# Sparse attention and feed forward: P by V behind the next scores, key copies and conversions dealt out in pieces

## The chip, the cores and the metric

The kernel runs on one core of a Trainium2 chip. A core has five engines that run at the same time, each with its own queue of instructions in program order: TensorE (PE; its weight loads are a row of their own, PEld), VectorE (DVE), ScalarE (ACT), GpSimd (POOL) and SyncE (SP). They wait for each other by semaphores. Data moves by DMAs, which SP, ACT and POOL issue. The metric is the device time of one execution in microseconds (us); less is better.

## What is computed

Block-sparse attention for 4 batches, 8 heads, 768 positions and 64 values a head, then a layer norm and a feed forward with a residual. In blocks of 32 positions, a query block sees its neighbours, the first and the last block, and three sampled blocks; the first and the last query block see all.

```python
scores = scale * np.matmul(q, k.transpose(0, 1, 3, 2))
...
mask = np.abs(blk_i - blk_j) <= window
mask = mask | (blk_i == 0) | (blk_j == 0) | (blk_i == n_blocks - 1) | (blk_j == n_blocks - 1)
for qb in range(n_blocks):
    for kb in sampled_blocks[qb]:
        mask[qb * block:(qb + 1) * block, kb * block:(kb + 1) * block] = True
scores = np.where(mask, scores, -1000000000.0)
...
attn = attn / (np.sum(attn, axis=-1, keepdims=True) + 1e-09)
return np.matmul(attn, v).astype(np.float32)
...
xn = (x - mu) / np.sqrt(var + 1e-06) * g_ln
ch = np.maximum(xn @ w_ch1, 0.0) @ w_ch2
return (x + ch).astype(np.float32)
```

The feed forward goes from 512 to 2048 and back.

## The kernel before

**Numbers.** Every fp32 operand of a matmul is held as two fp16 parts, a high and a low one (`qx`/`ql`, `pt[..., 0/1, :]`, `hh`/`hl`, `w1h`/`w1l`, `w2h`/`w2l`), and each product is three matmuls. To convert is a copy on ACT (high) and a subtraction on DVE (low): `convert_k` (L227, L228), `convert_v` (L241, L242), `convert_q` (L264 to L266), `convert_w` (L173 to L187; its ACT and DVE parts stand in the lists `whigh` and `wlow`, which `high()` and `low()` empty).

**Steps and units.** A batch has three units of two tiles of 128 positions: tiles (1, 2), (3, 4) and (0, 5) (`ORDER`). A step is four heads of one tile: 48 sparse steps, and 16 dense ones (`dense=True`) for the query blocks 0 and 23. A unit with tiles 0 and 5 has eight steps, the others four: 64 steps in all (`NS`). When a unit's steps are done its two tiles are normalised (`layer_norm`) and its feed forward (`ffn`) becomes available: 192 up matmuls (L523, eight groups of 24, each in one of three accumulators of the pool `ps_f`) and 96 down matmuls (L548). `hidden` takes a group's relu to fp16 (hh on ACT, L535; hl on DVE, L536); it is put into the program one group late (`late`).

**One step.** `scores` (L324) is 96 small matmuls (32 stationary columns, 64 or 96 moving ones); `softmax_max` (L368) and `softmax_exp` (L377); P is then split and transposed, in the first eight steps (`NPE`) by TensorE (`turn`, L382), later by SyncE's DMA transposes (`split_low`, L398); `attn_v` is P by V, 96 small matmuls (L431; dense: L458), with `finish` on DVE.

**Gathers.** The sampled keys are copied by ACT from the converted keys (`gather_k`, L281, twelve copies a step, by block numbers in registers). V is written in fp16 to a scratch tensor in DRAM (`vdr`) and fetched for a step by `gather_v` into one of three buffers `vg`: direct DMAs on SP (L290, L294) and one indirect DMA on POOL for each query block (L298, three or four a step). POOL holds little else. A buffer is free when the P by V of three steps before is done; that is what the indirect DMAs wait for.

**The order.** It is written out by hand, one iteration of the main loop for each step (L751 to L872). An iteration has a share of feed forward (`need`, `nff`), cut into eight parts, and `run(n)` puts n of its pieces into the program. `hook(i, p)` runs what was planned for point p of iteration i: conversions (`item`), V gathers (`at`), then loads that have room (`pump`). In the first eight iterations scores of step i + 1 come after P by V of step i - 1 and two parts of feed forward. From the eighth on: scores of step i, a part, the maximum, a part, exp, a part, the split, the key copies of steps i + 1 and i + 2 in one go (`keys`), a part, P by V of step i - 2 (`LAG`), then the other four parts, with the layer norm after the fifth; the V gather that the P by V frees stands at hook "d". The V gathers of the first three steps stand at the very start.

## Time and profile before

| what | us |
|---|---|
| median of 3 runs | 890.03 |
| lowest, highest of them | 887.67, 892.48 |
| the profiled execution, whole | 896.72 |
| its span, first to last instruction | 894.9 |
| TensorE matmuls busy | 742.4 |
| VectorE busy | 498.1 |
| ScalarE busy | 469.6 |
| GpSimd busy | 173.5 |

Busy time is the time in which an engine has an instruction under way; matmuls overlap one another, so a busy TensorE need not be at its peak. The granted clock is the share of full speed that TensorE had; its mean over the span was 0.931. Rows of the profile name an instruction by its line, engine and operation, and by output and inputs; "<-" behind an idle time names what ended it. "issue" stands where nothing that the profile shows ended it. Stages are read with windows of time, which list the busy time of each engine within them.

### The profile page before, as it was taken

What the parts mean: (1) busy time and instruction counts of PE and PEld (TensorE: products, weight loads), DVE (VectorE), ACT (ScalarE), POOL (GpSimd) and SP (SyncE); (2) the same over time, 40 slices, a digit from 0 to 9 for tenths busy, and PEclk for the clock granted to TensorE, in tenths of its full rate; (3) what the DMA queues carried; (4) which work ended last, traced back from release to release, by engine and by line L of the source; (5) the groups of instructions that cost most, each with busy time, mean ns of one, the idle gap of its engine ahead of it and who ended that gap; (6) DMA issues with size and microseconds to landing.
All of it is one profiled execution on the core that took longest, in us unless ns stands there. A gap on an engine that the chain in (4) does not pass through costs nothing.

```text
span 894.9 us, 31806 instructions
## 1 busy us (share of the span) xinstructions
PE 742.4 (83%) x13776; PEld 491.1 (55%) x13776; DVE 498.1 (56%) x900; ACT 469.6 (52%) x1201; POOL 173.5 (19%) x187
## 2 busy tenths in 40 slices
PE   0254486897878999997778999997778999999898
PEld 0143374375436748565435748575435748577483
DVE  4679977747654536446553536446463536435420
ACT  5655563346766655446745555446655654435020
POOL 0513110202232230111132230211132230111000
PEclk9999598998987999998977999998887999999999
DMA  8976553379677687587587698686587696466300
GB/s 288 285 244 200 163 158 123 114 175 225 132 168 169 144 181 163 148 189 158 114 144 154 141 181 159 151 185 161 109 144 158 142 176 129 105 118 112 72 1 24
DMA packets 196043, 136.70 MB, mean 153 GB/s; under 512 B 139584, under 2 KB 174912, under 8 KB 195904
## 3 DMA queue, kind: packets, MB, share of 16 engines
q1 hardware_dynamic: 186496, 110.69, 55.7%
q0 software_dynamic: 8448, 23.44, 9.9%
q8 instruction: 108, 1.77, 0.8%
q10 hardware_dynamic: 960, 0.54, 0.2%
q14 instruction: 31, 0.25, 0.1%
HBM read 89.18 MB, written 12.95 MB: 114 GB/s over the span
## 4 chain that ended last, share of the span: by engine, by line
PE 64%; DVE 13%; issue 10%; ACT 8%; DMA 3%; ACTq 1%; SPq 0%; DVEq 0%
PE pd L548 29%; PE pu L523 20%; PE ps L324 8%; PE pa L431 4%; ACT kg L281 3%; DVE st L368 2%; DVE hl L536 1%; ACT ps L377 1%; DVE kx L228 1%; PE pd L458 1%; DVE wf L175 1%; PE ps L382 1%; PE ps L355 1%; DMA w2l<-v 1%; ACT hh L535 1%
## 5 line engine op out<-in xcount | busy, mean ns | idle before, releaser
L523 PE MATMUL pu<-xT,w1h 128*128 128x256 f16 x1536 | 279.9, 284 | 21.6 <-DVE hl L536 10.3
L298 POOL DMA_INDIRECT vg<-vdr,vidx x176 | 172.9, 982 | 638.2 <-PE pa L431 412.5
L523 PE MATMUL pu<-xT,w1l 128*128 128x256 f16 x768 | 217.9, 284 | 0.0
L377 ACT ACTIVATE ps<-ps,st 128x256 f32<-128x256 f32 (+1 forms) x176 | 85.7, 487 | 200.5 <-DVE st L369 188.0
L523 PEld LDWEIGHTS <-w1h 128*128 128x128 f16 x1536 | 156.1, 102 | 51.3 <-DVE hl L536 11.9
L548 PE MATMUL pd<-w2h,hh 128*128 128x512 f16 x384 | 153.5, 400 | 5.8 <-DVE hl L536 5.6
L548 PE MATMUL pd<-w2l,hh 128*128 128x512 f16 x384 | 152.7, 398 | 0.0
L548 PE MATMUL pd<-w2h,hl 128*128 128x512 f16 x384 | 151.9, 396 | 0.0
L548 PEld LDWEIGHTS <-hh 128*128 128x128 f16 x768 | 73.0, 101 | 94.4 <-issue 13.0
L396 DVE TENSOR_TENSOR pw<-ps,pw 128x1024 f16<-128x1024 f32 (+1 forms) x56 | 64.3, 1149 | 108.0 <-ACT pw L389 99.7
L281 ACT COPY kg<-kx 128x128 f16 x576 | 119.4, 295 | 5.7 <-issue 3.6
L536 DVE SCALAR_TENSOR_TENSOR hl<-pu,hh 128x512 f16<-128x512 f32 x96 | 65.0, 687 | 80.6 <-ACT hh L535 74.3
L368 DVE TENSOR_REDUCE st<-ps 128x4 f32<-128x1024 f32 (+1 forms) x64 | 73.8, 1153 | 60.6 <-PE ps L324 58.9
L535 ACT ACTIVATE hh<-pu 128x512 f16<-128x512 f32 x96 | 54.8, 591 | 58.0 <-PE pu L523 51.4
L523 PEld LDWEIGHTS <-w1l 128*128 128x128 f16 x768 | 78.1, 102 | 12.6 <-issue 1.1
L324 PEld LDWEIGHTS <-ql 64*32 64x32 f16 x2304 | 34.9, 94 | 91.1 <-issue 69.4
L324 PE MATMUL ps<-kx,ql 64*32 64x64 f16 (+1 forms) x1536 | 46.3, 205 | 42.5 <-issue 22.6
L548 PEld LDWEIGHTS <-hl 128*128 128x128 f16 x384 | 39.1, 102 | 50.0 <-issue 8.3
L324 PE MATMUL ps<-kg,ql 64*32 64x96 f16 x768 | 42.2, 209 | 24.2 <-issue 18.3
L324 PE MATMUL ps<-kx,qx 128*32 128x96 f16 (+1 forms) x1536 | 44.4, 220 | 13.8 <-issue 13.8
L324 PEld LDWEIGHTS <-qx 128*32 128x32 f16 x2304 | 36.2, 107 | 32.8 <-issue 29.2
L389 ACT CAST pw<-ps 128x1024 f16<-128x1024 f32 (+1 forms) x56 | 53.3, 951 | 1.6
(80 smaller groups left out, 704.5 us busy)
## 6 DMA issues: line engine op xcount, KB each, us to landing
vg<-vdr SPq DMA_DIRECT2D x32, 390.0 KB
w2l<-w SPq DMA_DIRECT2D x13, 512.0 KB
va<-vdr SPq DMA_DIRECT2D x8, 780.0 KB
w2h<-w SPq DMA_DIRECT2D x12, 512.0 KB
out<-ot SPq DMA_DIRECT2D x24, 256.0 KB
qr<-qs SPq DMA_DIRECT2D x22, 256.0 KB
vdr<-vs SPq DMA_DIRECT2D x36, 130.0 KB
vg<-vdr SPq DMA_DIRECT2D x16, 292.5 KB
```

The lines of the kernel that those rows point to most:

```text
L281: nc.scalar.copy(kg[:, n], kxs[b, hg][:, :, bass.ds(val, 1)].rearrange("p j o q k -> p j (o q) k"))
L298: nc.gpsimd.indirect_dma_start(vg[:, qb - 4 * s.t, 1, :], None, src[:, :], bass.IndirectOffsetOnAxis(ap=vidx[:, qb : qb + 1], axis=0))
L324: nc.tensor.matmul(dst[:, at : at + n], stat, src[rows], start=first, stop=last, skip_group_check=True)
L368: nc.vector.tensor_reduce(out=s.st[:, 0 : s.m], in_=s.parts, axis=AX.X, op=ALU.max)
L377: nc.scalar.activation(to[:, k], s.parts[:, k], AF.Exp, bias=s.st[:, k : k + 1], scale=0.125)
L389: nc.scalar.copy(s.pw[:, 0, 0 : s.n], s.whole)
L396: nc.vector.tensor_sub(s.pw[:, 1, 0 : s.n], s.whole, s.pw[:, 0, 0 : s.n])
L431: nc.tensor.matmul(pa[gr * BLK : (gr + 1) * BLK, hl * 66 : hl * 66 + n], s.pt[:, ch + c, half, gr * BLK : (gr + 1) * BLK], s.vg[:, gr, c, ...
L523: nc.tensor.matmul(ph[:, j * 2 * P : (j + 1) * 2 * P], w[:, c, fs], xT[:, c, k, :], start=n == 0 and j == 0, stop=n == 3 * CT - 1, skip_gr ...
L535: nc.scalar.activation(dh, ph, AF.Relu)
L536: nc.vector.scalar_tensor_tensor(out=dl, in0=ph, scalar=0.0, in1=dh, op0=ALU.max, op1=ALU.subtract)
L548: nc.tensor.matmul(po, x[:, f, cols], w[:, f, :], start=f == 0 and n == 0, stop=f == FT - 1 and n == 2)
```

## The change

P by V moves, in the iterations from the eighth on, from after four parts of feed forward to after the first part; in the first eight, the scores of step i + 1 move ahead of P by V of step i - 1 (the order before had them behind two parts of feed forward and the split). The V gathers of steps 1 and 2 move from the start to behind the maximum of scores of steps 1 and 2, and GpSimd first copies four numbers of that maximum (`fence`), so that its indirect DMAs wait for it. `convert_k`, `convert_v`, `convert_q` and `gather_k` become generators; from the eighth iteration on `work` puts them into a list (`bg`), of which `tick` runs one piece: half a key or q conversion, one V conversion, four of the twelve key copies. `go(k)` puts a part of feed forward in two halves with a tick behind each; what is left runs at the iteration's end. `hidden` is put behind its own group at once, but for the first unit. The split moves behind the fourth part, the key copies (of step i + 2 alone) behind the fifth, and the three pieces of the layer norm behind the first, third and fourth part.

```diff
@@ -226,6 +226,7 @@
             rows, other = slice(j * D, (j + 1) * D), slice((1 - j) * D, (2 - j) * D)
             nc.scalar.copy(kx[rows, j, at], raw[rows])
             nc.vector.tensor_sub(kx[other, j, at], raw[rows], kx[rows, j, at])
+            yield
 
     def load_v(b, kt):
         if b == 0:
@@ -244,6 +245,7 @@
         for hg in range(HG):
             nc.sync.dma_start(vdr[b, hg][kt * P : (kt + 1) * P, :],
                               vs[:, hg * HL : (hg + 1) * HL].rearrange("p h d -> p (h d)"))
+        yield
 
     def load_q(b, t):
         if b == 0 and t in ORDER[0]:
@@ -264,6 +266,7 @@
             nc.scalar.copy(qx[rows, j], raw[rows])
             nc.vector.tensor_sub(ql[rows], raw[rows], qx[rows, j])
             nc.scalar.copy(qx[other, j], raw[rows])
+            yield
 
     vals = {}
 
@@ -279,8 +282,12 @@
         kgs[b, t, hg] = kg
         for n, val in enumerate(vals[b, t]):
             nc.scalar.copy(kg[:, n], kxs[b, hg][:, :, bass.ds(val, 1)].rearrange("p j o q k -> p j (o q) k"))
-
-    def gather_v(s):
+            if n % 4 == 3:
+                yield
+
+    fence = const.tile([1, 4], F32, name="fence")
+
+    def gather_v(s, behind=None):
         src = vdr[s.b, s.hg]
         vg = vp.tile([P, 4, 2, VW], F16, tag="vg", name=f"vg{s.i}")
         s.vg = vg
@@ -294,6 +301,8 @@
             nc.sync.dma_start(vg[3 * BLK : P, lo - 4 * s.t + a : lo - 4 * s.t + z, 0, :],
                               bass.AP(tensor=src.tensor, offset=src[at:, :].offset,
                                       ap=[[VW, BLK], [0, z - a], [1, VW]]))
+        if behind:
+            nc.gpsimd.tensor_copy(fence, behind.st[0:1, :])
         for qb in range(lo, hi):
             nc.gpsimd.indirect_dma_start(vg[:, qb - 4 * s.t, 1, :], None, src[:, :],
                                          bass.IndirectOffsetOnAxis(ap=vidx[:, qb : qb + 1], axis=0))
@@ -536,9 +545,13 @@
                 nc.vector.scalar_tensor_tensor(out=dl, in0=ph, scalar=0.0, in1=dh,
                                                op0=ALU.max, op1=ALU.subtract)
 
-            late.append(hidden)
+            if u.i == 0:
+                late.append(hidden)
+            else:
+                hidden()
             yield
-        late.pop()()
+        if late:
+            late.pop()()
 
         def down(po, k, f):
             while u.i == 0 and NW1 + f not in wready:
@@ -625,10 +638,30 @@
 
     gathered = set()
 
+    bg, regular = [], []
+
+    def tick():
+        if bg:
+            gen, end = bg[0]
+            if next(gen, "end") == "end":
+                bg.pop(0)
+                end()
+                tick()
+
+    def work(gen, end=lambda: None):
+        if regular:
+            bg.append((gen, end))
+        else:
+            for _ in gen:
+                pass
+            end()
+
     def keys(i):
         if i < NS and not steps[i].dense and i not in gathered:
             gathered.add(i)
-            gather_k(steps[i])
+            work(gather_k(steps[i]))
 
 
 
@@ -645,9 +678,15 @@
     def item(i, p, home, load, convert):
         n = index(i, p)
 
+        def free():
+            busy[home] -= 1
+
         def run_convert():
-            convert()
-            busy[home] -= 1
+            gen = convert()
+            if gen is None:
+                free()
+            else:
+                work(gen, free)
 
         loads.append((n, len(loads), home, load))
         hooks.setdefault(n, []).append(run_convert)
@@ -686,13 +725,13 @@
     tables_first()
     tables()
     for c in range(2):
-        convert_k(0, 0, c)
-    convert_q(0, first[0])
+        work(convert_k(0, 0, c))
+    work(convert_q(0, first[0]))
     for kt in range(3):
-        convert_v(0, kt)
-    gather_k(steps[0])
+        work(convert_v(0, kt))
+    keys(0)
     for kt in range(3, NT):
-        convert_v(0, kt)
+        work(convert_v(0, kt))
     WPOS = [None] * 3 + [(i, p) for i in range(1, 9) for p in PAT.get(i, "abcd")]
     WPOS = WPOS[:NW]
     assert len(WPOS) == NW
@@ -720,7 +759,8 @@
     for n, s in enumerate(order):
         fn = (lambda s=s: all_v(s.b, s.hg)) if s.dense else (lambda s=s: gather_v(s))
         if n < 3:
-            at(0, "pre", fn)
+            if n == 0:
+                at(0, "pre", fn)
         else:
             old = order[n - 3]
             i = place(old.i + 1 if old.dense else old.i)
@@ -767,25 +807,28 @@
             turn(s)
             if i == 0:
                 convert_w(0)
-                convert_k(0, 1, 0)
+                work(convert_k(0, 1, 0))
                 split_high(s)
                 high()
                 split_low(s)
-                convert_k(0, 1, 1)
+                work(convert_k(0, 1, 1))
                 keys(1)
                 convert_w(1)
-                convert_q(0, first[1])
+                work(convert_q(0, first[1]))
                 low()
                 matmul_scores(steps[1])
                 high()
                 convert_w(2)
                 keys(2)
                 softmax_max(steps[1])
+                gather_v(steps[1], steps[1])
                 low()
                 busy["raw"] = 0
             else:
                 hook(i, "a")
                 high()
+                if i < NPE - 1:
+                    matmul_scores(steps[i + 1])
                 tail = matmul_values(steps[i - 1])
                 need -= run(part[0] + part[1])
                 hook(i, "b")
@@ -793,8 +836,6 @@
                 split_high(s)
                 high()
                 split_low(s)
-                if i < NPE - 1:
-                    matmul_scores(steps[i + 1])
                 tail()
                 lns = norms(steps[i - 1])
                 for x in lns:
@@ -808,6 +849,8 @@
                     next(x)
                 if i < NPE - 1:
                     softmax_max(steps[i + 1])
+                if i == 1:
+                    gather_v(steps[2], steps[2])
                 need -= run(part[4] + part[5])
                 hook(i, "d")
                 low()
@@ -821,51 +864,58 @@
                 hook(i, "e")
                 hook(i, "f")
         else:
+            if not regular:
+                regular.append(True)
+
+            def go(k):
+                nonlocal need
+                n = part[k]
+                for m in range(2):
+                    need -= run(n * (m + 1) // 2 - n * m // 2)
+                    low()
+                    tick()
+                    high()
+
             if s:
                 matmul_scores(s)
-            need -= run(part[0])
-            lns = []
-            if i == NPE:
-                matmul_values(steps[i - 1])()
-                lns = norms(steps[i - 1])
+            go(0)
+            lns, tails = [], []
+            for n in [i - 1] * (i == NPE) + [i - LAG] * (i - LAG in range(NPE, NS)):
+                tails.append((matmul_values(steps[n]), steps[n]))
             if s:
                 softmax_max(s)
-            low()
+            for tail, x in tails:
+                tail()
+                lns += norms(x)
+            for x in lns:
+                next(x)
             hook(i, "a")
-            need -= run(part[1])
+            go(1)
             if s:
                 softmax_exp(s)
-            high()
-            need -= run(part[2])
-            low()
             hook(i, "b")
+            go(2)
+            for x in lns:
+                next(x)
+            go(3)
             if s:
                 split_high(s)
                 split_low(s)
-            keys(i + 1)
+            hook(i, "c")
+            for x in lns:
+                next(x, 0)
+            go(4)
             keys(i + 2)
+            hook(i, "d")
+            go(5)
+            hook(i, "e")
+            go(6)
+            hook(i, "f")
+            go(7)
+            while bg:
+                tick()
+            low()
             high()
-            need -= run(part[3])
-            low()
-            hook(i, "c")
-            if i - LAG in range(NPE, NS):
-                matmul_values(steps[i - LAG])()
-                lns += norms(steps[i - LAG])
-            high()
-            need -= run(part[4])
-            low()
-            for k in range(3):
-                for x in lns:
-                    next(x, 0)
-            hook(i, "d")
-            need -= run(part[5])
-            high()
-            hook(i, "e")
-            need -= run(part[6])
-            low()
-            hook(i, "f")
-            high()
-            need -= run(part[7])
             low()
         if not later and i >= NS + LAG + FFLAG:
             run(100000)
```

## The prediction

> **What bounds the kernel now.** I read the page first: the shares and the chain that ended last.
>
> ```profile
> span 894.9 us, 31806 instructions
> ...
> PE 742.4 (83%) x13776; PEld 491.1 (55%) x13776; DVE 498.1 (56%) x900; ACT 469.6 (52%) x1201; POOL 173.5 (19%) x187
> ...
> PE 64%; DVE 13%; issue 10%; ACT 8%; DMA 3%; ACTq 1%; SPq 0%; DVEq 0%
> ```
>
> TensorE is the bound, but 17% of the span it does nothing, a tenth of the chain is "issue" (a wait for nothing that the profile shows). So the question is where TensorE stands still. The list of waits names the scores (L324); I then asked for single blocks of scores, each 96 matmuls, by windows that just hold one (columns: window, its length, PE busy with count, PEld busy, clock, DMA share, GB/s).
>
> ```profile
> PE ps L324 <- issue: 63.0, 103, 1.9
> ```
> ```profile
> 426.00:427.30 1.30, 1.26 (x96) 1.11 (x96) 1.00 0.00 0
> 449.20:454.20 5.00, 2.67 (x96) 1.73 (x96) 0.77 0.91 230
> 462.60:467.50 4.90, 2.63 (x96) 1.79 (x96) 0.80 1.18 148
> 522.50:524.50 2.00, 1.46 (x96) 1.26 (x96) 1.00 0.94 210
> 574.80:576.00 1.20, 1.17 (x96) 1.11 (x96) 1.00 0.74 160
> ```
>
> The same 96 matmuls take 1.2, 2.0 or 5 us. Whether other DMAs run does not decide it (574.8 has a DMA share of 0.74 and is fast). GpSimd's rows for the same times do:
>
> ```profile
> 460.34 0.94 POOL L298 DMA_INDIRECT vg<-vdr,vidx  x1 [8.77 <-PE pa L431]
> ...
> 464.09 0.94 POOL L298 DMA_INDIRECT vg<-vdr,vidx  x1 [0.30 <-issue]
> ...
> 521.67 0.95 POOL L298 DMA_INDIRECT vg<-vdr,vidx  x1 [0.30 <-issue]
> ...
> 572.57 1.01 POOL L298 DMA_INDIRECT vg<-vdr,vidx  x1 [0.30 <-issue]
> ```
>
> Block 462.6 lies inside four indirect DMAs (460.34 to 465.03): 4.9 us. Block 522.5 begins 0.1 us before the last one ends (522.62): 2.0 us. Block 574.8 begins 1.2 us after the end (573.58): 1.2 us. So scores crawl while GpSimd issues indirect DMAs and for about 1 us after. The chain of waits shows the crawl, and that feed forward does not crawl (start, length, what):
>
> ```profile
> 449.70 0.33 issue
> ...
> 452.42 0.47 issue
> 452.90 1.43 PE ps L324 x56
> 454.33 4.88 PE pd L548 x12
> 459.21 0.84 PE pa L431 x72
> 460.05 2.70 PE pd L548 x12
> ...
> 481.26 7.69 PE pu L523 x48
> 488.94 0.89 PE pa L431 x96
> 489.83 5.35 PE pu L523 x48
> ```
>
> From 460.05, beside the indirect DMAs, twelve down matmuls take 2.70 us; after a crawl, with no indirect DMA left, the same twelve take 4.88. That second cost is the clock: after a crawl it is halved for some microseconds. By stages (columns: PE, PEld, DVE, ACT, POOL busy, then clock):
>
> ```profile
> 222.00:280.50 58.50, 47.06 (x1075) 26.14 (x1073) 33.53 (x64) 41.10 (x121) 18.04 (x18) 0.86 0.73 154
> 387.40:430.00 42.60, 33.91 (x708) 26.44 (x706) 26.74 (x47) 27.61 (x68) 6.45 (x6) 0.92 0.70 165
> 430.00:481.20 51.20, 41.69 (x793) 20.61 (x793) 24.59 (x49) 30.35 (x87) 15.12 (x16) 0.81 0.77 150
> 497.10:563.40 66.30, 64.60 (x1195) 45.58 (x1186) 34.67 (x61) 37.27 (x90) 14.38 (x15) 1.00 0.85 168
> 589.10:631.90 42.80, 33.41 (x707) 26.34 (x704) 26.59 (x47) 27.62 (x68) 6.44 (x6) 0.92 0.70 164
> 631.90:682.70 50.80, 41.27 (x793) 20.71 (x794) 24.53 (x49) 30.41 (x87) 15.25 (x16) 0.81 0.75 147
> 790.20:822.20 32.00, 30.74 (x710) 24.88 (x706) 17.55 (x37) 17.65 (x46) 5.67 (x6) 1.00 0.69 131
> ```
>
> Three stages alternate. **C** (222, 430, 632): an iteration has 24 down matmuls, twelve on each side of P by V; four sparse scores crawl in each. **A** (497): twice the feed forward, nearly full. **B** (387, 589, 790): 48 up matmuls an iteration; the third has no next batch to convert, and the same 710 matmuls take 32.0 us instead of 42.6 and 42.8.
>
> **The change part by part.**
>
> *P by V to behind the first eighth of feed forward.* The indirect DMAs wait for P by V (it frees their buffer). Four take 465.03 - 460.34 = 4.7 us and begin 0.3 us after P by V, so they end 5.0 us after it. In C, 21 of 24 down matmuls now follow: 21 x 2.70/12 = 4.7 us. The next scores would begin 0.3 us before the last indirect DMA ends, nearly the geometry of block 522.5. So a C block goes from 4.9 to 2.0 us: 12 x 2.9 = **34.8 us**. Bounds: 1.2 us if they miss each other (43 us in all), about 2.8 us if a second stall remains (25 us). In A, 84 of 96 up matmuls follow (84 x 5.35/48 = 9.4 us); the scores stand clear and go from 2.0 to 1.2: 12 x 0.8 = **9.6 us**. B's scores I count at nothing.
>
> Nothing new is waited for: P by V of a step comes two iterations after its scores, and its V was requested three P by Vs earlier. It is drawn ahead by three eighths of an iteration's feed forward, at most 4.0 us (36 x 5.35/48, in A), against two whole iterations (C: 51.2 us hold four). SyncE's direct V loads wait on the same buffer and stand later in program order than P by V, so what is queued behind them (q loads, P transposes, output stores) waits less.
>
> *The clock.* With crawls of under 1 us, as in A, where the clock is 1.00, C should run at full clock. In the second C stage four stretches of feed forward are slow:
>
> ```profile
> 441.03 4.38 PE pd L548 x12
> ...
> 467.66 5.04 PE pd L548 x12
> ```
>
> 4.38, 4.88, 5.04 against 2.70, and 7.69 against 5.35: 1.7 + 2.2 + 2.3 + 2.3 = 8.5 us. The other two by their clock: 8.4 (0.19 x 50.8 beside 0.19 x 51.2) and 7.2 (0.14 x 58.5). Of 24 us I take **21**; bounds 12 (half the stretches stay cold) and 24. The Trainium skill, "TensorE: Matmul & The Clock Gate", section "What's actually happening", puts the warm-up penalty below 1% of a typical kernel's span; by that the term would be at most 9 us, the forecast 12 us later. The trace disagrees: 8.5 us stand in one stage of 51.2 us.
>
> *Small pieces, hh and hl at once.* In B, TensorE stops for hh and hl; one of the three such waits of the second batch, and ACT's rows ahead of another:
>
> ```profile
> PE pd L548 <- DVE hl L536: 2.6, 1, 2.6
> ...
> 413.96 2.48 ACT L281 COPY kg<-kx 128x128 f16 x12
> 416.35 0.59 ACT L535 ACTIVATE hh<-pu 128x512 f16<-128x512 f32 x1
> ```
>
> hh stands behind twelve key copies (and hl behind it), and three accumulators cover two groups of 24 up matmuls, 5.35 us. The change issues hh right behind its matmuls and deals the copies out by four (0.8 us), a conversion by halves, two ticks in each eighth. The work stays: ACT has 27.6 us in B, 79% of 35. So the gap to the third B stage (10.6 and 10.8) closes, not wholly, as ACT is nearly full in the two iterations with both key conversions: 8 each, **16 us**; bounds 6 and 21. The first such stage (185 to 222) has one wait of 4.3 us:
>
> ```profile
> PE pu L523 <- DVE hl L536: 10.3, 4, 4.3
> ```
>
> I take **4 us** (0 to 5).
>
> *Start.* The gathers of steps 1 and 2 (eight indirect DMAs, 10 us of GpSimd, and SyncE's V loads with them) leave the head of the queues; the fence puts them behind the maximum of the scores that they would disturb. Scores go ahead of P by V, hence of the gathers that this frees. VectorE waits less:
>
> ```profile
> 46.96 1.23 DVE L368 TENSOR_REDUCE st<-ps 128x4 f32<-128x1024 f32 x1 [5.58 <-PE ps L324]
> ...
> 60.47 1.22 DVE L368 TENSOR_REDUCE st<-ps 128x4 f32<-128x1024 f32 x1 [2.04 <-PE ps L324]
> ...
> 50.00:115.00 65.00, 35.04 (x836) 26.05 (x837) 60.77 (x107) 37.93 (x101) 15.44 (x16) 0.82 0.62 188
> ```
>
> VectorE is 93% busy from 50 to 115 (weight conversion), so only its own waits count: 5.58 + 2.04 = 7.6. I take **7 us** (3 to 10). The fence's copy of four numbers on GpSimd and its wait hold up only the gathers behind it, needed one iteration later.
>
> *End.* The last unit waits for its normalised x behind the last P by V:
>
> ```profile
> 838.39 7.89 PE pd L548 x36
> ...
> 846.81 2.45 DMA xT<-xl
> ```
>
> Three eighths of 24 matmuls more (9 x 0.219 = **1.9 us**; 0 to 2) now cover that.
>
> **Sum.** 34.8 + 9.6 + 21 + 16 + 4 + 7 + 1.9 = 94.3 us. The profiled execution took 896.7 us (span 894.9): 802.4. The median of the runs shown is 890.0, 0.7% lower; scaled, **796 us**. Low ends of all terms: 25 + 8 + 12 + 6 + 0 + 3 + 0 = 54, so 836; high ends: 43 + 10 + 24 + 21 + 5 + 10 + 2 = 115, so 776.
>
> **Rivals.** *The forecast*, 785 to 812: chance 0.63.
>
> *Half kept*, 812 to 840, about 826: two stalls a block in C with the clock still falling, or ACT's backlog in B surfacing as new waits of the up matmuls. For it: in C the margin is -0.3 us, so any delay of the gathers is paid in the scores; for ACT, 79%. Against: in A one stall leaves the clock at 1.00. Chance 0.20.
>
> *More*, 772 to 785: C clears the gathers wholly. The margin speaks against it. Chance 0.10.
>
> *The crawl is the burst's own* (so many small matmuls outrun their supply of instructions, and P by V beside scores makes it worse). Then A, C, the clock and the start give nothing, and B, its first stage and the end 22 us: 874.8, scaled 868. Against: blocks 426.0 and 574.8 are the same burst in 1.2 us. Chance 0.04.
>
> *Slower.* Without the delay of one group, hh meets ACT's queue at its back: key copies, conversions and exp dealt out before it. If ACT ran more than the 5.35 us of two groups behind, each up group would wait. The eleven units have 88 groups; 1.1 us each eats the 94 us, 1.2 us (106 us) gives 908, scaled 902. Against: ACT is 52% busy, and the longest burst ahead of hh now is 2.48 us. Chance 0.03.
>
> A measurement of this kernel can tell about 0.5% from no change (4.5 us). Faster 0.95, the same 0.02, slower 0.03. All but the last rival, and that one's mild forms (0.02), are faster. The range of 776 to 836 leaves out the ends of both sides.
>
> **What would show it.** Scores blocks in C at 2.0 us and in A at 1.2; clock 0.95 or more in C; indirect DMAs ending at or before the next scores; first two B stages near 34 to 36 us; VectorE's wait of 5.6 us gone. I am wrong if scores crawl with no indirect DMA near them, if up or down matmuls crawl beside the gathers, if the clock still falls in C, or if "PE pu <- hl" grows.

## The result, and the profile after

The changed kernel takes 860.84 us (856.28 to 862.57, four runs) beside 890.70 (887.67 to 892.48) for the kernel before: ratio 0.966, interval 0.961 to 0.971. It is faster, but by a third of the forecast 94 us. The two profiled executions (896.72 and 856.28 us) lie 40 us apart, 10 more than the medians, so the stages below add up to 40. Two of the five runs of e1_move_alone, further down, were in a slower state (870.75 us, and 867.06, the profiled one); its ratio is of the other three. The page of the profiled execution (856.28 us), and its list of TensorE's waits (line, what ended them: us, times, longest):

```profile
span 854.4 us, 31756 instructions
...
PE 706.4 (83%) x13776; PEld 477.9 (56%) x13776; DVE 497.6 (58%) x900; ACT 465.5 (54%) x1201; POOL 174.9 (20%) x189
...
PE 59%; DVE 16%; ACT 12%; issue 7%; DMA 5%; SPq 1%; ACTq 0%; DVEq 0%
```
```profile
PE ps L333 <- DVE ql L267: 23.4, 9, 17.4
...
PE pa L440 <- issue: 17.9, 13, 3.3
PE ps L333 <- issue: 15.1, 24, 1.4
...
PE ps L333 <- ACT ps L386: 10.6, 2, 5.3
PE pu L532 <- DMA xT<-xh: 6.9, 3, 3.9
...
PE pd L467 <- issue: 4.9, 3, 3.1
```

The scores' "issue" fell from 63.0 us to 15.1, as the forecast wanted. New are "issue" inside P by V (17.9 and 4.9; before 0.2), and scores that wait for exp or for ql. Single blocks of scores (two in C, two in A) and the stages (columns as in the prediction):

```profile
431.20:433.80 2.60, 2.00 (x100) 1.36 (x99) 1.11 (x2) 0.00 (x0) 0.01 (x1) 1.00 1.47 143
440.20:442.80 2.60, 1.58 (x97) 1.31 (x98) 1.69 (x3) 2.48 (x5) 0.00 (x0) 1.00 0.23 66
484.50:485.70 1.20, 1.20 (x98) 1.09 (x96) 0.36 (x1) 1.20 (x8) 0.00 (x0) 1.00 0.84 176
498.40:499.60 1.20, 1.20 (x97) 1.10 (x96) 1.20 (x3) 1.20 (x8) 0.00 (x0) 1.00 0.96 215
```
```profile
377.00:407.10 30.10, 30.10 (x705) 24.63 (x704) 22.68 (x42) 21.36 (x49) 6.93 (x6) 1.00 0.82 208
407.10:450.50 43.40, 33.71 (x793) 18.46 (x792) 27.01 (x53) 31.09 (x90) 14.67 (x16) 0.92 0.78 145
484.50:552.80 68.30, 63.60 (x1138) 40.29 (x1137) 34.23 (x62) 35.20 (x91) 13.94 (x14) 1.00 0.75 151
```

B is full: 30.10 us busy of 30.10. Scores take 1.2 us in A, as forecast, and 2.1 to 2.7 in the second and third C (2.2 to 4.1 in the first), where 2.0 was forecast. Yet in the second C TensorE still stands for 9.7 of 43.4 us (the clock is 0.92; in the first and third C 0.90 and 0.88), and A lost ground. From the starts of the scores in the timelines, stage by stage (us; columns 3 and 5 are the same two kernels in the fourth set of runs, below):

| stage | before | after | before, set 4 | after, set 4 |
|---|---|---|---|---|
| start | 149.8 | 145.6 | 139.1 | 141.5 |
| first B-like stage | 55.6 | 46.4 | 56.0 | 46.7 |
| C, three stages | 52.5, 50.2, 50.0 | 51.3, 43.4, 43.2 | 43.1, 37.6, 37.9 | 52.0, 42.0, 41.7 |
| A, three stages | 111.0, 111.6, 111.3 | 116.3, 115.6, 111.8 | 113.2, 110.9, 112.3 | 112.5, 117.4, 115.2 |
| B, three stages | 39.9, 39.8, 31.8 | 30.2, 30.1, 30.1 | 39.7, 41.0, 31.4 | 30.9, 30.1, 30.1 |

### The profile page after: what moved, and what is told of

The parts are those of the page before. It is cut to its first block, busy times and chain, and to the rows that moved or that the text cites. A ratio compares the mean times of both kernels' runs of the same rounds, so it can differ in the third digit from the quotient of the medians.

```text
span 854.4 us, 31756 instructions
## 1 busy us (share of the span) xinstructions
PE 706.4 (83%) x13776; PEld 477.9 (56%) x13776; DVE 497.6 (58%) x900; ACT 465.5 (54%) x1201; POOL 174.9 (20%) x189
## 3 DMA queue, kind: packets, MB, share of 16 engines
q8 instruction: 108, 1.77, 0.9%
## 4 chain that ended last, share of the span: by engine, by line
PE 59%; DVE 16%; ACT 12%; issue 7%; DMA 5%; SPq 1%; ACTq 0%; DVEq 0%
PE pd L561 23%; PE pu L532 23%; PE ps L333 5%; PE pa L440 4%; ACT ps L386 3%; DVE st L377 2%; ACT kg L284 2%; DVE kx L228 1%; DVE wf L175 1%; ACT qx L266 1%; PE pd L467 1%; DMA xT<-xl 1%; DVE wf L177 1%; PE ps L364 1%; ACT qx L268 1%
## 5 line engine op out<-in xcount | busy, mean ns | idle before, releaser
L532 PE MATMUL pu<-xT,w1h 128*128 128x256 f16 x1536 | 274.2, 280 | 16.2 <-DMA xT<-xh 6.9
L532 PEld LDWEIGHTS <-w1h 128*128 128x128 f16 x1536 | 153.5, 100 | 42.1 <-issue 10.6
L561 PE MATMUL pd<-w2h,hh 128*128 128x512 f16 x384 | 148.2, 386 | 0.8 <-DVE hl L545 0.8
L561 PE MATMUL pd<-w2l,hh 128*128 128x512 f16 x384 | 147.9, 385 | 0.0
L561 PE MATMUL pd<-w2h,hl 128*128 128x512 f16 x384 | 147.4, 384 | 0.0
L493 ACT ACTIVATE mv<-mv,eps 128x1 f32<-128x1 f32 x24 | 7.1, 294 | 149.2 <-DVE mv L492 141.3
L333 PE MATMUL ps<-kx,ql 64*32 64x64 f16 (+1 forms) x1536 | 39.0, 209 | 42.7 <-DVE ql L267 23.4
L333 PEld LDWEIGHTS <-ql 64*32 64x32 f16 x2304 | 31.4, 96 | 72.3 <-DVE ql L267 37.3
L440 PE MATMUL pa<-vg,pt 128*32 128x65 f16 (+1 forms) x4224 | 52.0, 202 | 17.9 <-issue 17.9
L440 PEld LDWEIGHTS <-pt 128*32 128x32 f16 x4224 | 44.8, 100 | 34.8 <-issue 33.4
L567 DVE SCALAR_TENSOR_TENSOR ot<-pd,x 128x512 f32<-128x512 f32 x24 | 16.4, 688 | 64.6 <-PE pd L561 64.6
```

Source lines behind the costliest of these rows:

```text
L333: nc.tensor.matmul(dst[:, at : at + n], stat, src[rows], start=first, stop=last, skip_group_check=True)
L440: nc.tensor.matmul(pa[gr * BLK : (gr + 1) * BLK, hl * 66 : hl * 66 + n], s.pt[:, ch + c, half, gr * BLK : (gr + 1) * BLK], s.vg[:, gr, c, ...
L532: nc.tensor.matmul(ph[:, j * 2 * P : (j + 1) * 2 * P], w[:, c, fs], xT[:, c, k, :], start=n == 0 and j == 0, stop=n == 3 * CT - 1, skip_gr ...
L561: nc.tensor.matmul(po, x[:, f, cols], w[:, f, :], start=f == 0 and n == 0, stop=f == FT - 1 and n == 2)
L567: nc.vector.scalar_tensor_tensor(out=ot, in0=po, scalar=1.0 / (SW1 * SW2), in1=xs[u.b, t], op0=ALU.mult, op1=ALU.add)
```

## The experiments

Each set of runs was made on one chip, beside its own runs of the kernel before. In sets 1, 2 and 5 that takes 889 to 892 us; in sets 3 and 4, on two other chips, 854 to 855. So a kernel is compared within its set, or by its ratio.

| set, before | kernel | median (range), us | ratio, interval |
|---|---|---|---|
| 1, 891.64 | e1_move_alone | 858.59 (854.17 to 870.75) | 0.960, 0.957 to 0.963 |
| | e3_pv_third | 856.54 (852.25 to 860.64) | 0.960, 0.956 to 0.965 |
| | e4_exp_first | 855.33 (848.84 to 858.97) | 0.957, 0.952 to 0.961 |
| | e5_direct | 859.16, one run | |
| 2, 888.93 | e2_pv_back | 867.82 (864.02 to 873.07) | 0.978, 0.972 to 0.983 |
| | e7_shift | 844.02 (842.58 to 845.46) | 0.949, 0.946 to 0.952 |
| | e8_place | 846.65 (842.82 to 848.98) | 0.953, 0.951 to 0.955 |
| | e9_place_early | 819.57 (816.47 to 821.91) | 0.922, 0.920 to 0.925 |
| 3, 853.61 | e6_pool_direct | 848.59, one run | |
| | e10_early_pad | 818.23 (815.10 to 818.78) | 0.958, 0.953 to 0.962 |
| | e11_shift64 | 843.45 (841.41 to 847.33) | 0.990, 0.985 to 0.995 |
| | e12_early_pv_back | 822.49 (820.95 to 823.75) | 0.964, 0.959 to 0.969 |
| 4, 854.80 | r1_before (the kernel before) | 857.06 (853.29 to 859.93) | 1.002, 0.998 to 1.006 |
| | r2_after (the changed kernel) | 851.39 (847.34 to 854.40) | 0.995, 0.992 to 0.999 |
| | r3_early (as e9) | 817.25 (815.98 to 818.49) | 0.956, 0.950 to 0.962 |
| | r4_early_back (as e12) | 826.66 (824.38 to 827.57) | 0.967, 0.961 to 0.973 |
| 5, 891.21 | r5_early_back (as e12) | 855.20 (851.06 to 858.99) | 0.961, 0.956 to 0.965 |
| | r6_pool_direct (as e6) | 851.33, one run | |

**The parts alone.** To the kernel before only the move of P by V:

```
             need -= run(part[0])
...
+            for n in [i - 1] * (i == NPE) + [i - LAG] * (i - LAG in range(NPE, NS)):
+                tails.append((matmul_values(steps[n]), steps[n]))
...
-            if i - LAG in range(NPE, NS):
-                matmul_values(steps[i - LAG])()
```

> The kernel before, with P by V alone moved behind the first eighth of feed forward (from the eighth iteration on); start, conversions, key copies and hh/hl as before. Three theories of why the change gave 30 us and not 94. SUPPLY: TensorE's instructions come in pages of 256, a page takes some 3.6 us, and scores with P by V close behind outrun it. Then the same stalls of 1 to 3.5 us inside or just behind P by V appear here as in the changed kernel (there 20, 28 us in all), the A stages grow by 4 us each although their scores fall to 1.1 us, and the time is 865 to 880. ACT ORDER: the loss comes from exp standing behind the layer norm and the dealt-out conversions in ScalarE's queue. Here neither is dealt out, so P by V does not stall, A gains 3 us a stage, C 15 us a stage, and the time is below 845. NO CRAWL: scores do not crawl because of the gathers; then the C scores stay near 4.7 us.

The time lies between what the first two theories gave. And in the changed kernel P by V behind the fourth part again, the rest left:

```
             go(3)
...
+            if i - LAG in range(NPE, NS):
+                tails.append((matmul_values(steps[i - LAG]), steps[i - LAG]))
```

> The changed kernel with P by V put back behind the fourth part and layer norm behind part 4; pieces, immediate splits of the hidden layer and the new start stay. Theory (two costs: the scores crawl beside the indirect DMAs, and TensorE waits for pages of 256 instructions when scores and P by V come in one burst): the waits 'issue' in P by V lines go (from 28 us in all to under 5), 'issue' in the scores rises from 15 to some 50 us as before the change, the dense stages B keep what they gained (30 us each, not 40); in all 862 to 880 us. Rival (the pieces gain nothing by themselves, the move alone makes the gain, as the run of the move alone suggests): 885 to 893. Rival (the late indirect DMAs cost nothing): about 845, faster than the changed kernel.

The move alone gains 4.0%, the rest alone 2.2%, both 3.4%: they do not add up. With P by V back the scores' "issue" is 41.0 us, and "issue" in P by V 13.8 (22.8 in the changed kernel); 9.8 of the 13.8 stand before the first matmul of four P by Vs, not inside. The first two B stages take 33.8 us, not the 30 expected.

**Is it the indirect DMA?** Fixed rows in place of sampled ones, from SyncE's queue and from GpSimd's:

```
-            nc.gpsimd.indirect_dma_start(vg[:, qb - 4 * s.t, 1, :], None, src[:, :], ...
+            nc.sync.dma_start(vg[:, qb - 4 * s.t, 1, :], src[0:P, :])      # e5
+            nc.gpsimd.dma_start(vg[:, qb - 4 * s.t, 1, :], src[0:P, :])    # e6, r6
```

> The kernel before with each indirect DMA on GpSimd replaced by a direct DMA on SyncE of the same size from fixed rows (the sampled rows of V are left out). If scores crawl because GpSimd issues indirect DMAs, all sparse scores take about 1.1 us, C runs at full clock, and the time falls by about 43 + 21 + 10 + 7, to about 810 (SyncE has 80 us more to issue, which may give some of it back). If the crawl belongs to the bytes or the packets, or to the burst itself, scores in C stay at 4 to 5 us and the time near 890.

> The kernel before with each indirect DMA replaced by one of the same size issued on the same queue of POOL from fixed rows (so the sampled rows of V are left out). If the crawl of the scores comes from what POOL does to issue an indirect DMA: a POOL instruction here is far shorter than the 0.94 us of before and 'issue' in front of the scores falls from 63 us to under 15, as with the issue on SP. If it comes from the small descriptors of the queue that POOL feeds: the instructions get shorter and the scores still lose some 40 to 60 us.

> The kernel before with DMAs of fixed rows on POOL's queue in place of the indirect ones (the sampled rows of V are left out), where the crawl is: if the gather by index is its source, 'issue' in front of the scores falls from some 63 us to under 15 and the time to 845 to 860 us; if the queue of POOL is, it stays at 40 us or more and the time over 875 us. On a chip without the crawl about 848 us again, which tells nothing.

The waits of e5 and of r6, one row each:

```profile
PE ps L323 <- issue: 7.7, 7, 1.6
PE ps L323 <- issue: 11.3, 7, 3.7
```

The scores' "issue" falls from 63.0 us to these, and r6 takes 851.33 us beside 891.21. With e5 the time was expected at about 810 and is 859.16: its three C are 39.1 us shorter than those of the kernel before, its three A 7.1 us longer. Two blocks of scores of r6, and GpSimd's rows ahead of them:

```profile
418.30:419.60 1.30, 1.30 (x97) 1.11 (x96) 1.18 (x6) 1.30 (x8) 0.00 (x0) 1.00 1.01 215
427.70:429.00 1.30, 1.30 (x97) 1.11 (x96) 0.69 (x1) 0.82 (x2) 0.00 (x0) 1.00 2.07 191
```
```profile
416.07 2.12 POOL L298 DMA_DIRECT2D vg<-vdr  x4 [22.57 <-PE pd L457]
425.44 2.12 POOL L298 DMA_DIRECT2D vg<-vdr  x4 [7.25 <-PE pa L430]
```

Four direct DMAs cost GpSimd 2.12 us instead of 4.7 and are issued before the scores begin; the transfers themselves do not slow them. Whether scores beside the issue of direct DMAs would crawl is thus not seen.

**The crawl depends on the chip.** In set 3, e12_early_pv_back had only 2.5 us of "issue" before its scores, with P by V at its old place. So the kernel before was profiled in set 4:

> The kernel before once more, unchanged, for its trace on the chip of these runs, since in the last runs it took 853.6 us there and not 890. Theory (what differs between chips is the crawl of the scores beside the indirect DMAs): where it takes some 890 us the waits 'issue' in front of its scores come to 55 to 70 us, where it takes some 854 to under 20 us, and the difference of these waits is the difference of the times within 10 us. Rival (a chip differs in something else, its DMA or its clock): the waits 'issue' are about 63 us on either, and another row differs.

> The changed kernel unchanged, on the same chip. Theory: where the kernel before takes 890 us, 858 to 862 us again; where it takes 854, 840 to 850 us, since the move of P by V has no crawl to end there and leaves its page waits.

Blocks of its scores in C, GpSimd's rows around the second, its waits:

```profile
420.20:421.50 1.30, 1.30 (x97) 1.14 (x96) 0.24 (x1) 0.00 (x0) 0.95 (x1) 1.00 0.87 177
427.90:430.60 2.70, 2.25 (x97) 1.57 (x96) 2.00 (x6) 2.64 (x8) 1.89 (x2) 1.00 1.17 192
436.80:439.00 2.20, 2.07 (x97) 1.50 (x96) 2.05 (x7) 0.80 (x5) 1.71 (x2) 1.00 1.17 221
```
```profile
426.89 0.94 POOL L298 DMA_INDIRECT vg<-vdr,vidx  x1 [0.30 <-issue]
428.14 0.95 POOL L298 DMA_INDIRECT vg<-vdr,vidx  x1 [0.30 <-issue]
429.39 0.95 POOL L298 DMA_INDIRECT vg<-vdr,vidx  x1 [0.30 <-issue]
```
```profile
PE pu L523 <- DVE hl L536: 21.6, 10, 4.5
...
PE ps L324 <- issue: 9.0, 7, 2.4
...
PE pa L431 <- issue: 5.7, 5, 1.9
```

The same indirect DMAs, of the same 0.94 us, lie beside the scores, which take 1.3 to 2.7 us, not 4.9. The time differs by 894.9 - 855.2 = 39.7 us of span, the scores' "issue" by 54.0, not the same within 10 us as expected: what a crawl holds up is partly late anyway (hl: 21.6 us here, 10.3 where the scores crawl). So by these two chips some 40 us is an estimate of all that ending the crawl could win. The changed kernel runs at 851.39 there: where nothing crawls the whole change is worth 0.5%.

**TensorE waits for its instructions.** The longest new stall, in the chain of waits of the changed kernel (start, us, what), lies in P by V of a step of A:

```profile
321.36 1.24 PE ps L333 x75
322.60 1.42 PE pu L532 x12
324.01 0.53 PE pa L440 x52
324.54 3.27 issue
327.82 0.57 PE pa L440 x43
328.39 10.83 PE pu L532 x84
```

The page's queues name what comes then:

```profile
q8 instruction: 108, 1.77, 0.9%
```

TensorE has 13776 matmuls and as many weight loads; with the 83 waits that the trace has in its queue they are 27635 instructions, 107.9 pages of 256, and 1.77 MB in 108 packets are 16.4 KB each. Numbered, waits included, in the order of their starts, every stall inside P by V (behind its first matmul) of over 0.3 us from one start to the next that waits for nothing else, 16 of 16, stands at a number that leaves 193 when divided by 256, and ends 1.2 to 1.6 us after a packet of this queue has landed; no two packets land less than 3.2 us apart. These are 19.6 of the 22.8 us of "issue" in P by V; the other 3.15 us stand before the first matmul of a P by V, at another number, behind a wait for a semaphore. The Trainium skill, "Runtime: NRT & Kernel Launch", section "Instruction fetch mechanics", has instructions come in such blocks of 256, which agrees, and calls the cost of a boundary mostly hidden, which does not hold for this burst: 192 instructions of scores, 24 of feed forward and 192 of P by V begin within some 3.5 us.

Such stalls are not the move's alone. They are 8.7 of the 9.0 us of the scores' "issue" in r1_before and all of it in e5 and r6, and r1 has 5.5 us of them in P by V, at its old place. So next to nothing is left of the crawl's own "issue" in these three, and where the crawl ends, part of its price comes back as waits for pages.

The next run moves every page against the program by half its length:

```
+                for _ in range(64):
+                    nc.tensor.matmul(pad[0:32, 0:64], qpad[:, 0, 0, 0:32], qpad[:, 0, 0, 0:64],
+                                     start=True, stop=True)
```

> The changed kernel with 64 tiny matmuls (128 instructions of TensorE with their weight loads) added in its first step, where TensorE waits for exp; nothing else differs. Theory (TensorE stalls where a page of 256 instructions is not there yet): the stalls of over 0.7 us in P by V and behind it leave the places where they stand now (in the step of the scores at 321.3 the 3.5 us stall in P by V goes, likewise 2.0 us in that at 512.2, 2.25 us behind that at 696.8, 2.4 us in that at 128.5) and stand 128 instructions earlier or later in other bursts; their number stays at 10 to 25 and the time within 1% of the changed kernel. Rival (what P by V waits for is its operand, PSUM or the sampled rows): the stalls stay in the same steps at the same matmuls, with lengths within 0.3 us.

```profile
291.58 1.24 PE ps L333 x75
292.82 1.40 PE pd L561 x6
294.22 0.85 PE pa L440 x92
295.07 1.71 issue
...
318.86 1.24 PE ps L333 x75
320.10 1.42 PE pu L532 x12
321.52 0.94 PE pa L440 x96
```

The step that stalled 3.3 us runs through, an earlier one that ran through now stalls, and all 9 such stalls in P by V again leave 193. The time was expected within 1% and fell by 1.7%, 844.02 against 0.966 x 888.93 = 859. In the whole kernel 12 stalls for pages are left of 20, 20.2 us of 28.1 from start to start, and the three stages of A give 9.6 of the 15 us (111.7, 110.2, 112.2). C is 13.8 us shorter, where the scores' wait for exp fell from 10.6 us to 1.6, and B 11.6 us longer. So about half of the 15 us lies in the stalls themselves. Two more phases:

> The changed kernel with 32 tiny matmuls, 64 instructions, instead of the 64 that made it 16 us faster. Theory (phase of the pages): at this phase some 25 bursts of scores and P by V meet the end of a page, against 26 without and 20 with the first shift, so the time is that of the changed kernel or above, 855 to 870 us, with the stalls at other matmuls again. Rival (the added matmuls help by themselves, by keeping TensorE busy early): about 844 to 852, half or all of the gain again.

> The fastest kernel so far (P by V placed by the number of pieces, exp first, conversions early) with 96 tiny matmuls, 192 instructions, added in its first step. Theory (the phase of the pages of 256 instructions against the bursts sets which bursts stall): all stalls of over 0.3 us in P by V stand at other matmuls than without the addition, and the time moves by up to 10 us either way, by the sum of the stalls; by the list of bursts, slightly fewer of them meet a page at this phase: 810 to 822 us. Rival (phase does not matter, the gain of the first shift came from its place): within 2 us of 819.6.

The stalls moved again (15 and 13 in P by V, all leaving 193). Their sets had no crawl, so the times expected cannot be held against them; beside set 4 they are 0.990 to 0.995 (the intervals touch) and 818.23 to 817.25 us. So the phase always sets where a stall stands. A gain of 1.7% is seen in e7 alone, whose set has no run of the changed kernel beside it; that the added matmuls help by themselves (the rival of e11) isn't excluded. Another way to part the burst is P by V behind the third eighth (with exp straight behind max):

```
             go(2)
...
+            for n in [i - 1] * (i == NPE) + [i - LAG] * (i - LAG in range(NPE, NS)):
+                tails.append((matmul_values(steps[n]), steps[n]))
```

> The changed kernel with P by V behind the third eighth of feed forward instead of the first, exp straight behind the maximum, and the layer norm's pieces after both. SUPPLY: between scores and P by V now lie 3.9 us of feed forward in A, 2.0 us in C; the stalls in P by V vanish in A (about 16 us) and shrink in C; the gathers end 1.3 us later in C, so its scores rise from about 2.1 to 3.5 us. Sum about 845 to 855. ACT ORDER: stalls in P by V stay as they are; the waits of the up matmuls for xT (9.3 us) and of scores for exp and ql (some 14 us) shrink because exp and its split come earlier; about 840 to 850 with P by V still stalling. The place of the stalls in the instruction stream (always the same modulo 256, or not) tells them apart.

The sparse steps in the middle of A come to 12.7 to 13.0 us but for one of 14.2 (12.7 to 17.9 in the changed kernel), but C's scores crawl again (28.2 us of "issue"), and the total, 856.54, stays above the 845 to 855 expected. So it belongs behind the third eighth in A and behind the first in B and C (exp stays straight behind max):

```
+            thick = nff > 60
...
+            if thick:
+                values()
+                finishes()
```

> The changed kernel with exp straight behind max, and P by V behind the first eighth where an iteration has 48 pieces of feed forward and behind the third eighth where it has 96. Theory (page supply decides in the 96-piece stages, ACT's order in the others): steps of the 96-piece stages at 12.7 to 12.9 us instead of 13.5 to 14.8 and stalls under 10 us in all; the 48-piece stages as in the run with exp first; 838 to 848 us. Rival (what was saved by either alone returns as waits for the q conversion): 853 to 858.

`nff` is the pieces of feed forward in an iteration: 96 in A, 48 in B and C. "Issue" in P by V falls to 10.4 us, the time to 846.65.

**ACT's order.** In the changed kernel the second batch's C begins with a wait of 5.3 us for exp. ACT's rows:

```profile
413.47 2.49 ACT L284 COPY kg<-kx 128x128 f16 x12
415.86 0.60 ACT L544 ACTIVATE hh<-pu 128x512 f16<-128x512 f32 x1
416.35 0.61 ACT L266 CAST qx<-qr 64x512 f16<-64x512 f32 x1
416.99 0.62 ACT L268 CAST qx<-qr 64x512 f16<-64x512 f32 x1
417.62 0.61 ACT L266 CAST qx<-qr 64x512 f16<-64x512 f32 x1
418.26 0.62 ACT L268 CAST qx<-qr 64x512 f16<-64x512 f32 x1
418.91 1.89 ACT L386 ACTIVATE ps<-ps,st 128x256 f32<-128x256 f32 x4
```

ACT has no gap: exp stands behind the pieces, and its scores' buffer comes free late. First, exp straight behind max:

```
                 softmax_max(s)
+                softmax_exp(s)
...
             go(1)
-            if s:
-                softmax_exp(s)
```

> The changed kernel with one edit: exp stands straight behind the maximum, ahead of the layer norm's pieces and of the dealt-out conversions in ScalarE's queue; P by V stays behind the first eighth. SUPPLY: the stalls in P by V stay (about 28 us in all), so at most the waits for xT (9.3 us) and part of those for exp and ql (14 us) go: 840 to 855. ACT ORDER: everything lost in A and C comes back: below 830, P by V at 0.8 us.

```profile
PE ps L333 <- DVE ql L267: 40.7, 10, 16.9
```

The wait for exp went, and came back as one for ql (23.4 us became 40.7, of which the start has 16.9): ACT was late by the same work. So the work must come earlier (on top of e8):

```
-        for hg, i in ((0, f - 4), (1, f - 3)):
+        for hg, i in ((0, f - 6), (1, f - 4)):
...
-                    item(*((s.i - 2, "a") if s.i <= NPE else (s.i - 1, "a")), "raw", ...
+                    item(*((s.i - 2, "a") if s.i <= NPE else (s.i - 2, "d")), "raw", ...
```

> The kernel with P by V placed by the number of pieces and exp first, and besides the key conversions of the next batch's first half two iterations earlier, of its second half one earlier, and the q conversions one iteration earlier. Theory (the first scores of each batch wait for the q conversion that stands behind the key conversions in ACT's queue): the wait of the scores for ql in the three 48-piece stages falls from some 8 us a stage to under 2, and the kernel is 12 to 20 us faster than with the placing alone: 822 to 834 us. Rival (the conversions crowd the 96-piece stage in their turn): within 5 us of the placing alone.

```profile
PE ps L333 <- issue: 17.9, 28, 1.2
PE ps L333 <- DVE ql L267: 16.6, 1, 16.6
...
PE pa L440 <- issue: 8.5, 7, 3.5
```

All waits for ql but the start's are gone (40.3 us in e8, 16.6 here), and the time falls by 27 us to 819.57, 7.8% under the kernel before, the largest gain of all ratios. With these edits but P by V behind the fourth part (and exp first, as in e9), the place of P by V is priced on both kinds of chip:

> The kernel with exp first and the conversions one to two iterations early, but P by V back behind the fourth part. It prices the move of P by V once ACT's order is out of the way. Theory (the move ends the crawl of the scores, some 23 us of 41, and costs the waits for pages): 835 to 845 us, the 48-piece stages at 10 to 11 us a step instead of 8.5 to 9. Rival (the early conversions make the whole gain, the move none): within 5 us of 819.6.

> The kernel with P by V placed by the number of pieces, exp first, conversions early, unchanged, on the same chip: 817 to 822 us where the kernel before takes 890; where it takes 854, 803 to 818 us (its scores lose 18 us to 'issue', which go).

> The same with P by V behind the fourth part, on the same chip. Theory (on a chip with the crawl the move of P by V is worth some 20 us by itself once ACT's order is mended; without the crawl it is worth nothing): 835 to 850 us where the kernel before takes 890, 820 to 825 us where it takes 854. Rival (the move is worth nothing anywhere): within 4 us of the kernel with P by V placed by the number of pieces on either.

> The kernel with conversions early, exp first and P by V behind the fourth part again, in the hope of a chip on which the kernel before takes some 890 us. Theory (with the crawl, P by V beside the scores is what ends it, and is worth some 20 us once ACT's order is mended): 835 to 850 us there, with 25 to 45 us of 'issue' in front of the scores, against 819.6 with P by V placed by the number of pieces. Rival (the early conversions make the whole gain): within 5 us of 819.6. On a chip without the crawl: 822 to 827 us again, and the question stays open.

The first of these was expected on a chip with the crawl and met one without it. Without the crawl the place of P by V is worth 826.66 - 817.25 = 9 us, where nothing was expected (set 3, 822.49 and 818.23, has 4, its second kernel with added matmuls); with it, the ratios 0.961 and 0.922 differ by 0.038, or 34 us, above the 20 expected; r5 itself came out above its 835 to 850. In r5 the scores crawl (4.1 us, beside 1.89 us of GpSimd):

```profile
417.60:421.70 4.10, 1.94 (x97) 1.53 (x96) 1.17 (x2) 2.68 (x5) 1.89 (x2) 1.00 0.38 112
428.20:432.40 4.20, 2.06 (x97) 1.51 (x96) 3.00 (x8) 4.18 (x15) 1.89 (x2) 1.00 0.82 183
```

The kernel with both mended takes 819.57 where scores crawl and 817.25 where they do not: next to nothing of the crawl is left in the time.

## Why the prediction was right, and where it failed

- *B, its first stage, the end.* Right in kind, and more than forecast. Forecast 16 + 4 + 1.9; by the table B gained 9.8 and 9.6, the first stage 9.2 (its bounds were 0 to 5), the third B and what follows it 2.7. The pieces alone (e2) have 6.1, 6.0 and 3.8; the rest comes with P by V's new place, which was counted at nothing in B.
- *The start.* Right in kind: 4.2 us of 7.
- *The crawl as a cause.* Right where it exists: e5 and r6 take the indirect DMAs away and it goes. Scores came to 1.2 us in A as forecast; the twelve blocks of C fell by 27.6 us in all, inside the bounds of 25 and 43 but not the 34.8.
- *Its price, "12 x 2.9 = 34.8 us" and the clock's "21", together 56 in C.* Mis-sized. With the crawl gone C is 9.4 + 12.6 + 12.2 = 34.2 us shorter in set 4, 28.7 in r6 and 39.1 in e5. The two terms were added as if all that a crawl delays were on the path; part is made up by waits that it hides, as hl's and those for pages. The same holds for A's 9.6: with its scores at 1.3 us, A is 2.5 us longer in r1, 7.1 longer in e5 and 8.5 shorter in r6. The clock, named at 0.95 or more in C, came to 0.92 at best.
- *"Nothing new is waited for."* This step failed. It asked after data and buffers and left out two things in the same queues. TensorE's instructions: P by V right behind the scores makes a burst that outruns their supply, 19.6 us of stalls for pages in P by V instead of 0.2. ACT's order: exp and the q conversions stand behind pieces that come due in the same iterations. So C gave 14.8 us, about half of what it could, and A, with 13.9 us of stalls for pages, lost 9.7 where 9.6 was forecast. e8 and e9 mend the two, and the time falls to 819.57. Of the 94.3 us forecast the profiles show 40.5: C is 41 short, A 19, the start 3, and B with the end is 9 over.
- *Rivals.* "Half kept" named ACT's backlog, as a wait of the up matmuls; it came as one of the scores. "The crawl is the burst's own" (0.04) was wrong on the crawl, but its mechanism, a burst that outruns its instructions, is real: it stood in the prediction as all or nothing and was left out of the sum.
- *The range.* Its low-gain end summed the low ends of gains; it held no price for a new wait beside them, and 860.84 lies 25 us above it.

Why the move alone is as fast as the whole change isn't settled. By e1's one profile (867.06 us) its three C take 122.9 us, 15.0 less than in the changed kernel, its three A 341.4 against 343.6, the four B-like stages 158.2 against 136.8 and the start 152.0 against 145.6. This suggests that what the rest of the change wins in B and at the start it gives back in C, where conversions stand ahead of exp in ACT's queue. e1 has the stalls for pages too, 19.9 us of "issue" in P by V, so they come with the move.

## What to carry to other kernels

Before hundreds of small matmuls are put next to each other, count instructions, not only busy time: here 400 in 3.5 us outrun pages of 256 that landed at least 3.2 us apart, and some 4 us of large matmuls between the groups in A (e8) left 9 of the 20 stalls, 10.1 of 28.1 us. When work is dealt out in pieces, list what stands ahead of the one instruction that the bound engine waits for; moving that instruction up only moves the wait, starting the work an iteration earlier removes it. A price read off a stall is an upper bound: what the stall hides comes due when it goes.

## What the runs showed of the hardware

- Sparse scores with 1.7 to 1.9 us of GpSimd's indirect DMAs beside them took 4.9 and 5.0 us in C on one chip (the prediction's blocks 462.6 and 449.2) and 2.2 and 2.7 on another (r1), with the same program and the same 0.94 us for an indirect DMA. The kernel before takes 890.7 - 854.8 = 36 us longer on the former. Why the chips differ stays open.
- A stall for a page in P by V lasted up to 3.3 us in the changed kernel, and 128 added instructions at the head of the program, which do nothing for the result, moved every such stall. The time fell by 15 us, by the ratios of two sets; about half of that lies in the stalls.
